# Start and last sequence of a fused Fourier-layer and MLP kernel: whole products and unread ones in the first rounds, a second tile for the mixed rows, a closer step for the last sequence

## The chip, the cores and the metric

The program runs on one core of a Trainium2 chip. The metric is the device time of one execution in microseconds (us), as the median of several runs. TensorE is called PE, VectorE DVE, ScalarE ACT and GpSimd POOL; SP is the engine whose queue issues every DMA of this kernel.

## The reference

Eight sequences of 3136 rows and 256 columns go through a Fourier layer and then a second layer with an MLP, all in fp32:

```python
X = np.fft.rfft(x, axis=1)
Yr = Xr @ w_r - Xi @ w_i + b_r
Yi = Xr @ w_i + Xi @ w_r + b_i
Yr = np.sign(Yr) * np.maximum(np.abs(Yr) - lam, 0.0)     # Yi the same
y = np.fft.irfft(Y, n=x.shape[1], axis=1)
# second layer, x = y
mixed = np.real(np.fft.fft(np.fft.fft(x, axis=1), axis=2))
u = x + mixed
un = (u - mu) / np.sqrt(var + 1e-06)                     # over the 256 columns
out = u + np.maximum(un @ w_ch1, 0.0) @ w_ch2
```

## The kernel before

A sequence of 3136 rows is seen as 64 x 49. Its transform goes in two stages. **F1** (`p1`, `p1_first`) multiplies 64-row slices by a table of cosines and sines and writes the result to DRAM (`ad`; for sequence 0 `a0`, `a8`, `ad0`). **F2** (`p2_f2`, line 531) reads it back as `af`, multiplies it with the table tile `tff`, and splits the result into a high part in fp32r and a remainder (`Xh`, `Xl`, `Xsh`, `Xsl`). A sequence has four quarters q of 8 frequencies u, each with four such products `ui`. **W** (`p2_w`) makes the three complex weight products, 18 matmuls for each half o of the columns. From its result Y one branch (`p2_yt`, `p2_g2`) goes back by the inverse table to DRAM (`bd`), the other (`p2_mix`, tile `mq`) forms the mixed rows and writes them to DRAM (`md`). **G1** (`p3_norm`) reads `bd` as `bf`, ends the inverse transform and adds the mixed rows, read from `md` as `mt`, into `ut`. `p3_tr` transposes `ut`, and `p3_mlp1` and `p3_mlp2` are the MLP (tiles `h` and `o`). A group of the MLP is four (or three) pairs of rows; a sequence has six or seven groups.

Both F1 and G1 contract over 64 rows only, for two halves at once. `quads` writes such a round as four products of 64x64 each, which fill two PSUM tiles; `pair` first clears a column of both tiles by two small DVE memsets (line 322), and `run_quads` (lines 329, 334) lets the products wait for both memsets. A round of F1 of sequence 2 and later can wait in `waiting` for the round of G1 of an older sequence and goes out with it: a joint round. The first sequence uses the whole 128x128 table at once (line 370).

The order is written by a planner: every generator yields virtual times, T = 10000 to a sequence, a heap runs the earliest, and a scheduler then places each engine's instructions. Every engine and SP work their queues in order. Sequence b has its steps of W, mix and G2 at `clock2`, with `STEP` = 0.25 T per quarter (0.13 for sequence 0), and its groups at `clock3`. The MLP weights come as 64-bit floats: `weights` loads them in eight pieces `raw_w` of 512 KB and `split_double` turns each into a pair of fp32r tiles, mostly on DVE (`cv_w`, lines 181 to 199). w1 goes from 1.14 T on in steps of 0.065 T, w2 from 1.73 T on. Pieces 5 and 6 load into the tags `uth` and `utl`, which before hold the split of the odd quarters of sequence 0.

Four PSUM buffers (`gtile`) are shared by all of F1, F2, W, mix, yt, G2, G1 and the transposes; `h` and `o` have two each. `mt` has one buffer and is loaded by four DMAs per group (line 800), `ev` (the result of F1 on its way to DRAM) has four, `im` two.

Of the kernel before, what the change touches and what calls it, by code (L numbers as in the profile page):

```python
# [10 lines left out]
F32 = mybir.dt.float32  # L11
F32R = mybir.dt.float32r
# [15 lines left out]
S = 50  # L28
# [92 lines left out]
T = 10000  # L121
# [7 lines left out]
W_AT, W_STEP = 1.14, 0.065  # L129
W2_AT, W2_STEP = 1.73, 0.07  # L130
MLAG, NRM, TR = 0.874, -1.239, -0.993
TURN = 0.2


@with_exitstack
def spectral_block(ctx: ExitStack, tc: tile.TileContext, x, w_ri, b_ri, w1, w2,
# [31 lines left out]
    UTB, EVB = 7, 4  # L168
# [47 lines left out]
    def load_consts():  # L216
# [6 lines left out]
        wi = sb.tile([128, 2, D], F32, tag="mt", bufs=1, name="wi")  # L223
# [36 lines left out]
    mean_m = cp.tile([128, 128], F32R, name="mean_m")  # L260
    va.memset(mean_m.bitcast(F32), 1.0 / D)
# [76 lines left out]
    def p1_first():  # L338
# [21 lines left out]
        for ci, (m, n) in enumerate(todo):  # L360
# [9 lines left out]
            te.matmul(g[:, :w], fwd_0, xf[:, i * 512:i * 512 + w], start=True, stop=True)  # L370
# [32 lines left out]
    def p1(b):  # L403
# [32 lines left out]
        for k, t in enumerate(times):  # L436
            yield t
            while b == 1 and (0, 1, 1) not in f2_mm:
                yield now[0] + 10
            if k + 1 < len(times):  # L440
                load(k + 1)
            xf = xfs.pop(k)
            if k == 6:
                gs = [gtile("g_f1")]
                te.matmul(gs[0][:, :D], fwd_f, xf[:, :D], start=True, stop=True)
            else:
                gs, marks = pair("g_f1")
                ops = quads(gs, fwd_f, xf.rearrange("q (p i d) -> q p i d", p=2, d=D))
                key = keys[k] if b > 1 else None
                if key is None:  # L450
                    with tc.issue_after(f2_mm[0, 1, 1]) if b == 1 and k == 0 else nullcontext():
                        run_quads(ops, marks)
                else:
                    waiting[key] = ops, marks
                    yield t + 2
                    while key in waiting:
                        yield now[0] + 10
            for r, g in enumerate(gs):
                ev = sb.tile([128, 512], F32, tag="ev", bufs=EVB, name="ev")
                w = D if k == 6 else 512  # L460
                (va.tensor_copy if r else sc.copy)(ev[:, :w], g[:, :w])
                for p in range(2):
                    ad, n2, n = (a_dram[b + p](0)[0], N2 - 1, 1) if k == 6 else (a_dram[b](0)[0], 8 * k + 4 * r + 2 * p, 2)
# [27 lines left out]
    def p2_f2(b):  # L491


        for q in range(4):
# [5 lines left out]
            afs, tfs = [], []  # L500
            for s in range(2):
# [10 lines left out]
                tff = sb.tile([98, 4, 100], F32, tag="eo" if roomy else "tff", bufs=2 if roomy else 3, name="tff")  # L512
                nc.sync.dma_start(out=tff, in_=c_tf[:, u0 + 4 * s:u0 + 4 * s + 4, :])
                afs.append(af)
                tfs.append(tff)
# [3 lines left out]
            for ui in range(4):  # L519
# [34 lines left out]
                else:  # L554
                    im = sb.tile([128, 2, 2 * S], F32, tag="im", bufs=2, name="im")
# [219 lines left out]
    def p3_norm(b):  # L775

        def load_bf(gi):
# [12 lines left out]
        def load_mt(g0, z):  # L790

            mt = sb.tile([128, 4, D], F32, tag="mt", bufs=1, name="mt")
            n0, odd = 2 * g0, g0 + z == NM
            n = 2 * (z - odd)
            for p in range(2):
                for h, (d, back) in enumerate(zip(m_dram[b], (False, True))):
                    v = d[0:NH].rearrange("(a n2) d -> a n2 d", n2=N2)
                    v = v[:, N2 - n0 - n:N2 - n0][:, ::-1] if back else v[:, n0:n0 + n]
                    o = mt[64 * p + 32 * h:64 * p + 32 * h + 32, :n // 2]
                    nc.sync.dma_start(out=o, in_=v.rearrange("a (t p) d -> p a t d", p=2)[p])  # L800
                    if odd:
# [24 lines left out]
        for gi, (g0, z) in enumerate(groups[b % 2]):  # L826
            t0, T3 = clock3(b, g0)
            if gi:
                yield t0 + T3 * (NRM - 0.25)
# [18 lines left out]
            mine = {}  # L848
# [76 lines left out]
    def weights():  # L925
# [13 lines left out]
        yield T * (W_AT - W_STEP)  # L939
# [21 lines left out]
    tasks = [load_small(), load_consts(), weights()]  # L961
# [47 lines left out]
```

## Time and profile before

| | |
|---|---|
| median of 3 runs | 1890.32 us (1889.23 to 1893.35) |
| the profiled execution | 1888.82 us |
| its span, first to last instruction | 1887.0 us |
| PE busy | 1815.6 us (96%) |
| DVE, ACT, POOL busy | 1211.3 us (64%), 820.9 us (44%), 404.9 us (21%) |
| chain that ended last | PE 88%, DMA 5%, DVE 3%, SP's queue 2% |

The page cuts the span in 40 slices; PE is busy 9 tenths or more of each but the first, second and fourth (5, 7 and 5 tenths). So the reader should look at two places, the first 195 us, up to the first product of the MLP, and the few later points at which PE waited. "Granted clock" is the share of PE's full clock that the chip gave in a stretch: 1.00 is 2.4 GHz, 0.50 is 1.2 GHz, and a mean between them is time at either level.

### The profile page before, as it was taken

The page shows a single profiled execution, that of the slowest core. Times are in us where ns is not written, and L with a number is a line of the kernel's source. Part 1 is how long each engine was busy: PE and PEld are TensorE (multiplying, and loading weights), DVE is VectorE, ACT ScalarE, POOL GpSimd, SP SyncE. Part 2 cuts the span into 40 slices and gives each one's busy share as a digit, 9 for nine tenths or more (in the row PEclk, how much of TensorE's full clock was granted, in tenths as well). Part 3 has the DMA queues.
Part 4 walks back from the last instruction along what each step waited for, and adds up shares of the span by engine and source line. Part 5 has one row for each costly group of instructions (what it writes and reads, how often), then busy time and mean ns, then how long its engine had stood idle before and what let it go on. Part 6 is the DMA issues. An engine that isn't in the chain of part 4 may idle for free.

```text
span 1887.0 us, 34092 instructions
## 1 busy us (share of the span) xinstructions
PE 1815.6 (96%) x12344; PEld 1620.0 (86%) x12344; DVE 1211.3 (64%) x2853; ACT 820.9 (44%) x1839; POOL 404.9 (21%) x858
## 2 busy tenths in 40 slices
PE   5795999999999999999999999999999999999999
PEld 3673889989889988898899988988989998987898
DVE  2665777767667766666766676666667666655443
ACT  2564544444445444444444444444444443432222
POOL 0444222222222112322112222211222221211000
PEclk7896999999999999999999999999999999999999
DMA  7768453355345535354354554345435432232110
GB/s 203 206 174 237 131 148 114 102 147 158 102 119 155 153 107 137 103 141 129 102 148 125 158 141 116 92 124 152 120 86 141 126 92 69 68 109 86 53 35 26
DMA packets 155581, 232.94 MB, mean 123 GB/s; under 512 B 19022, under 2 KB 110742, under 8 KB 155414
## 3 DMA queue, kind: packets, MB, share of 16 engines
q1 hardware_dynamic: 155414, 230.78, 44.4%
q8 instruction: 97, 1.59, 0.4%
q14 instruction: 70, 0.57, 0.1%
HBM read 127.95 MB, written 102.76 MB: 122 GB/s over the span
## 4 chain that ended last, share of the span: by engine, by line
PE 88%; DMA 5%; DVE 3%; SPq 2%; issue 1%; ACT 1%; POOL 0%; DVEq 0%; ACTq 0%
PE o L157 10%; PE o L158 9%; PE h L157 9%; PE h L158 9%; PE h L159 9%; PE o L159 9%; PE g_f L531 5%; PE g_w L157 3%; PE g_w L159 3%; PE g_w L158 3%; PE g_yt L727 3%; PE g_ut L877 2%; PE g_g L329 2%; PE g_mix L658 2%; PE g_g L157 1%; PE g_f L334 1%
## 5 line engine op out<-in xcount | busy, mean ns | idle before, releaser
L899 DVE SCALAR_TENSOR_TENSOR hl<-h,hh 128x512 fp32r<-128x512 f32 (+1 forms) x416 | 273.6, 658 | 378.0 <-ACT hh L898 377.0
L898 ACT ACTIVATE hh<-h 128x512 fp32r<-128x512 f32 (+1 forms) x416 | 238.6, 574 | 462.9 <-PE h L159 427.9
L158 PE MATMUL o<-w2h,hl 128*128 128x256 f32 x1568 | 432.2, 285 | 1.2 <-DVE hl L899 1.1
L159 PE MATMUL o<-w2h,hh 128*128 128x256 f32 x1568 | 423.2, 280 | 0.0
L157 PE MATMUL o<-w2l,hh 128*128 128x256 f32 x1568 | 399.9, 288 | 0.0
L157 PE MATMUL h<-utl,w1h 128*128 128x512 f32 (+1 forms) x832 | 323.6, 389 | 0.0
L158 PE MATMUL h<-uth,w1l 128*128 128x512 f32 (+1 forms) x832 | 318.5, 383 | 0.0
L159 PE MATMUL h<-uth,w1h 128*128 128x512 f32 (+1 forms) x832 | 318.2, 382 | 0.0
L157 PEld LDWEIGHTS o<-w2l,hh 128*128 128x128 f32 x1568 | 283.3, 189 | 33.7 <-issue 17.9
L158 PEld LDWEIGHTS o<-w2h,hl 128*128 128x128 f32 x1568 | 296.3, 189 | 7.9 <-issue 2.4
L159 PEld LDWEIGHTS o<-w2h,hh 128*128 128x128 f32 x1568 | 296.5, 189 | 2.8 <-issue 0.8
L817 POOL TENSOR_SCALAR vv<-ag 128x2 f32<-128x2 f32 x104 | 20.5, 197 | 728.8 <-DVE ag L814 714.1
L159 PEld LDWEIGHTS h<-uth,w1h 128*128 128x128 f32 x832 | 156.5, 188 | 23.7
L157 PEld LDWEIGHTS h<-utl,w1h 128*128 128x128 f32 x832 | 157.0, 189 | 17.3 <-DVE hl L899 2.4
L158 PEld LDWEIGHTS h<-uth,w1l 128*128 128x128 f32 x832 | 157.0, 189 | 16.3 <-issue 3.2
L531 PE MATMUL g_f<-tff,af 98*128 98x100 f32 x1024 | 149.9, 281 | 14.9 <-DMA tff<-c_tf 9.4
L531 PEld LDWEIGHTS g_f<-tff,af 98*128 98x128 f32 x1024 | 141.8, 200 | 24.6 <-issue 10.6
L154 POOL TENSOR_TENSOR Xl<-xx,Xh 128x400 fp32r<-128x400 f32 (+1 forms) x96 | 102.0, 1064 | 165.5 <-ACT Xh L545 128.2
L600 ACT ACTIVATE r<-g_w,two_t 128x400 f32<-128x400 f32 x128 | 76.2, 596 | 98.7 <-DVE g_w L596 89.6
L154 POOL TENSOR_TENSOR Xsl<-xs,Xsh 128x200 fp32r<-128x200 f32 x120 | 80.0, 669 | 121.7 <-ACT Xsh L545 116.9
L596 DVE SCALAR_TENSOR_TENSOR g_w<-g_w,bias,ks 128x400 f32<-128x400 f32 x128 | 81.3, 636 | 37.0 <-PE g_w L159 31.0
L673 POOL TENSOR_TENSOR mq<-mq 100x508 f32<-100x508 f32 x31 | 43.5, 1404 | 279.7 <-DVE mq L671 234.1
(155 smaller groups left out, 3364.2 us busy)
## 6 DMA issues: line engine op xcount, KB each, us to landing
bd<-bev SPq DMA_DIRECT2D x128, 196.0 KB
out_dram<-ut SPq DMA_DIRECT2D x92, 256.0 KB
af<-ad SPq DMA_DIRECT2D x60, 392.0 KB
ad<-ev SPq DMA_DIRECT2D x176, 128.0 KB
xf<-in_x SPq DMA_DIRECT2D x86, 256.0 KB
md<-mq SPq DMA_DIRECT2D x112, 192.0 KB
bf<-bd SPq DMA_DIRECT2D x80, 256.0 KB
mt<-md SPq DMA_DIRECT2D x160, 128.0 KB
```

The lines of the kernel that those rows point to most:

```text
L154: gp.tensor_sub(out_, full, hi.bitcast(F32))
L157: te.matmul(o, lh, rl, start=start, stop=False)
L158: te.matmul(o, ll, rh, start=False, stop=False)
L159: return te.matmul(o, lh, rh, start=False, stop=stop)
L329: mm = te.matmul(*ops[0], start=True, stop=True)
L531: f2_mm[b, q, ui] = te.matmul(o, afs[s][:, ui * D + k * 128:ui * D + k * 128 + 128], tfs[s][:, ui].rearrange("p (c j) -> p c j", c=2), sta ...
L596: va.scalar_tensor_tensor(gw, gw, bias[:, c, o:o + 1], ks, op0=ALU.add, op1=ALU.add)
L600: sc.activation(r, gw, AF.Relu, bias=lam_t)
L673: me.tensor_add(mq[:, 0, :, 0, 1:], even[:, :, 1:], odd[:, :, 1:])
L727: te.transpose(gt[:100, (v * 2 + o) * 128:(v * 2 + o + 1) * 128], y[:, o, place].rearrange("p c j -> p (c j)"), ident)
L898: sc.activation(hh[:, :w], h[:, :w], AF.Relu)
L899: va.scalar_tensor_tensor(hl[:, :w], h[:, :w], 0.0, hh[:, :w].bitcast(F32), op0=ALU.max, op1=ALU.subtract)
```

## The change

1. Products that nobody reads: `keep_busy(n)` issues n products of 128x512 of a constant tile into a PSUM tile of tag `o`: 8 ahead of the first F1 product, 14 behind the fourth, 32 behind the last of F1 of sequence 0, and 14 behind F2 of its first quarter, 68 in all.
2. All six F1 rounds of sequence 1, three of sequence 2 and the first group of G1 of sequence 0 use the whole 128x128 table: two products of 128x512 (18 for F1, 2 for G1), without memsets, each with its own evacuation. They come at 1.235 T and on in steps of 0.034 T, the first behind the fourth F2 product of quarter 1 (`FIRST`). Sequence 2 has three early rounds of its own (`EARLY`, before two) and three joint ones (before four).
3. In a joint round ScalarE copies both F1 tiles; before, it copied one and VectorE the other.
4. The first two table tiles `tff` are loaded ahead of the first stores; w1 starts at 1.27 T in steps of 0.055 T.
5. `mt` has two buffers and is loaded half a group's time ahead instead of a quarter; the first group's is loaded in two pieces (8 DMAs of 64 KB), and G1 of that group runs piece by piece. `ev` has three buffers, `im` one.
6. The quarters of the last sequence stand 0.235 T apart instead of 0.25 T.

```diff
-W_AT, W_STEP = 1.14, 0.065
+W_AT, W_STEP = 1.27, 0.055
+EARLY, HALF = (1.66, 1.775, 1.885), 0.058
+FIRST, F1_AT, F1_STEP = (0, 1, 3), 1.235, 0.034
-    UTB, EVB = 7, 4
+    UTB, EVB = 7, 3
+    def load_tf():
+        yield 0.95 * T
+        for s in range(2):
+            tff = sb.tile([98, 4, 100], F32, tag="tff", bufs=3, name="tff")
+            behind("x", out=tff, in_=c_tf[:, 4 * s:4 * s + 4, :])
+            first_tf.append(tff)
+    def keep_busy(n, last=None):
+        o = ps.tile([128, 512], F32, tag="o", bufs=2, name="o_idle").rearrange("p (a k) -> p a k", k=128)
+        m = mean_m.rearrange("p (a k) -> p a k", a=1).to_broadcast((128, 4, 128))
+        for _ in range(n):
+            with tc.issue_after(last) if last is not None else nullcontext():
+                last = te.matmul(o, mean_m, m, start=True, stop=True).ins
...
-            te.matmul(g[:, :w], fwd_0, xf[:, i * 512:i * 512 + w], start=True, stop=True)
+            if ci == 0:
+                keep_busy(8)
+            mm = te.matmul(g[:, :w], fwd_0, xf[:, i * 512:i * 512 + w], start=True, stop=True)
+            if ci == 3:
+                keep_busy(14, mm.ins)
+            if ci == len(todo) - 1:
+                keep_busy(32, mm.ins)
...
-            times = [T * (1.18 + 0.07 * k) for k in range(6)]
+            times = [T * (F1_AT + 2 * F1_STEP * k) for k in range(6)]
-            times = {g1_time(c, gi): (c, gi) for c in range(b) for gi in range(len(groups[c % 2]))}
-            times.update({T * 1.62: None, T * 1.71: None})
+            times = {g1_time(c, gi): (c, gi) for c in range(b) for gi in range(len(groups[c % 2])) if c + gi}
+            times.update({T * t: None for t in EARLY})
...
+            whole = k == 6 or b == 1 or keys[k] is None
...
+                if whole:
+                    yield t + (F1_STEP if b == 1 else HALF) * T * r
+                    g = gtile("g_f1")
+                    with tc.issue_after(f2_mm[FIRST]) if b == 1 and k == r == 0 else nullcontext():
+                        te.matmul(g[:, :w], fwd_f, xf[:, r * 512:r * 512 + w], start=True, stop=True)
-                (va.tensor_copy if r else sc.copy)(ev[:, :w], g[:, :w])
+                (va.tensor_copy if r and whole else sc.copy)(ev[:, :w], g[:, :w])
...
-        step = T * ((STEP0, STEP1)[b] if b < 2 else STEP)
+        step = T * ((STEP0, STEP1)[b] if b < 2 else STEP if b < NB - 1 else 0.235)
-                    im = sb.tile([128, 2, 2 * S], F32, tag="im", bufs=2, name="im")
+                    im = sb.tile([128, 2, 2 * S], F32, tag="im", bufs=1, name="im")
+                if b == q == o == 0:
+                    keep_busy(14, f2_mm[0, 0, 3])
...
-            mt = sb.tile([128, 4, D], F32, tag="mt", bufs=1, name="mt")
+            mt = sb.tile([128, 4, D], F32, tag="mt", bufs=2, name="mt")
+            cuts = (0, 4, 8) if b == g0 == 0 else (0, n)
-                yield t0 + T3 * (NRM - 0.25)
+                yield t0 + T3 * (NRM - 0.5)
+            if b == gi == 0:
+                for i, n in parts_of[z]:
+                    yield max(now[0], g1_time(b, gi) + T3 * i / 4)
+                    g = gtile("g_g1")
+                    with behind_w(1, i == 0):
+                        te.matmul(g, inv_f, bf[:, i * D:i * D + 512], start=True, stop=True)
+                    ut = mine[i] = sb.tile([128, 2, D], F32, tag="ut", bufs=UTB, name="ut")
+                    va.tensor_add(ut, g.rearrange("p (n d) -> p n d", d=D), mt[:, i:i + n])
...
-        yield T * (W_AT - W_STEP)
+        yield T * (W_AT - 2 * W_STEP)
```

How this stands in the built programs is shown at three places. The first is PE's order behind W of quarter 0, first half (sequence 0): `g_f<-tff,af` is F2 of quarter 1, `g_f<-xf` is F1 of sequence 1, `g_w` is W. Before:

```order
L531 MATMUL g_f_395<-tff,af 128x2x50 x4
L531 MATMUL g_f_412<-tff,af 128x2x50 x4
L329 MATMUL g_f_433<-xf,fwd_f 64x512
L334 MATMUL g_f_433<-xf,fwd_f 64x512
L334 MATMUL g_f_432<-xf,fwd_f 64x512 x2
L531 MATMUL g_f_448<-tff,af 128x2x50 x4
L157 MATMUL g_w<-Xsl,wrh 128x400
```

With the change, behind three F2 products (12 matmuls) and the first six matmuls of W:

```order
L159 MATMUL g_w<-Xl,wsh 128x400
L160 MATMUL g_w<-Xh,wsl 128x400
L161 MATMUL g_w<-Xh,wsh 128x400
L159 MATMUL g_w<-Xl,wsh 128x400
L160 MATMUL g_w<-Xh,wsl 128x400
L161 MATMUL g_w<-Xh,wsh 128x400
L561 MATMUL g_f_519<-tff,af 128x2x50 x4
L482 MATMUL g_f_525<-xf,fwd_f 128x512
L159 MATMUL g_w<-Xl,wdh 128x400
```

The first F1 product of sequence 1 now stands behind all four F2 products of quarter 1 and behind 12 matmuls of W, where before it stood behind two F2 products and ahead of W.

The second place is DVE's order where it reaches the first piece of w2 (`raw_w2`); `g_f1` are PSUM tiles of F1 of sequence 2, `mq` the mixed rows of sequence 0. Before:

```order
L322 MEMSET g_f1_1396 128x1
L186 TENSOR_SCALAR cv_w2_ut_1424<-raw_w2_1353 128x512
L322 MEMSET g_f1_1397 128x1
L182 TENSOR_SCALAR cv_w2_hh_1420<-cv_w2_hh_1420 128x512
L677 COPY mq_1133<-mq_1133 100x4x127
```

With the change:

```order
L703 TENSOR_TENSOR mq_1164<-mq_1164 100x4x64 x2
L188 TENSOR_SCALAR cv_w2_ut_1449<-raw_w2_1391 128x512
L184 TENSOR_SCALAR cv_w2_hh_1445<-cv_w2_hh_1445 128x512
L186 TENSOR_SCALAR cv_w2_hh_1445<-cv_w2_hh_1445 128x512
L184 TENSOR_SCALAR cv_w2_hh_1557<-cv_w2_hh_1557 128x512
L189 TENSOR_TENSOR cv_w2_ut_1449<-cv_w2_ut_1449,cv_w2_hh_1445 128x512
L186 TENSOR_SCALAR cv_w2_hh_1557<-cv_w2_hh_1557 128x512
L709 COPY mq_1164<-mq_1164 100x4x127
L700 TENSOR_TENSOR mq_1381<-g_mix_1417,mq_1381 100x1
```

The memset of an F1 tile no longer stands behind the first read of a piece of w2; an evacuation of a mix tile (line 700) still does. On SP the pieces of w2 are issued as 1353, 1355 before and as 1393, 1391 with the change, so the piece that DVE reads first is now the second of the two.

The third place is PE's order ahead of the first transposes of the last sequence (`g_ut<-ident,ut`, which need its mixed rows). Before:

```order
L158 MATMUL h<-uth,w1l 128x512
L159 MATMUL h<-uth,w1h 128x512
L157 MATMUL h<-utl,w1h 128x512
L158 MATMUL h<-uth,w1l 128x512
L159 MATMUL h<-uth,w1h 128x512
L157 MATMUL o<-w2l,hh 128x256 x2
L877 MATMUL g_ut<-ident,ut 128x128 x8
```

With the change:

```order
L159 MATMUL h<-utl,w1h 128x512
L160 MATMUL h<-uth,w1l 128x512
L161 MATMUL h<-uth,w1h 128x512
L159 MATMUL h<-utl,w1h 128x512
L160 MATMUL h<-uth,w1l 128x512
L161 MATMUL h<-uth,w1h 128x512
L923 MATMUL g_ut<-ident,ut 128x128 x8
```

Between the last mix product of the last sequence and these transposes stand 24 matmuls of `h` and 62 of `o` before, 36 and 72 with the change. At the same place of sequence 6 it is 35 of `h`, 47 of `o` and 6 of G2 before, 48, 63 and 12 with the change; at sequences 2 and 4 nothing moves (48, 54 and 6).

## Rows read from the trace of the kernel before

**Rows 1.** Stretches: start:end, us, busy (x) PE, PEld, DVE, ACT, POOL, PEclk, DMA share, GB/s

```profile
0.00:56.00 56.00, 30.68 (x96) 21.04 (x100) 15.81 (x37) 16.18 (x37) 5.87 (x13) 0.77 0.80 210
0.00:194.85 194.85, 135.89 (x654) 103.67 (x655) 107.58 (x231) 91.68 (x220) 73.58 (x86) 0.81 0.77 206
31.48:47.28 15.80, 12.51 (x48) 12.20 (x49) 3.07 (x7) 4.70 (x13) 4.33 (x6) 0.50 0.87 237
1499.00:1510.00 11.00, 9.79 (x64) 9.55 (x65) 7.93 (x25) 4.29 (x11) 2.27 (x11) 0.84 0.79 204
1697.00:1710.00 13.00, 8.88 (x50) 6.96 (x50) 6.07 (x19) 2.65 (x6) 1.65 (x10) 0.87 0.32 89
```

**Rows 2.** Chain that ended last, single steps: start us, us, engine, what, line

```profile
38.55 6.22 DMA af<-a
91.03 0.87 PE g_f L531 x8
95.73 0.61 PE g_f L329
96.39 0.38 PE g_f L329
109.04 0.95 PE g_mean L269 x4
1775.57 0.43 PE g_g L845 x2
```

**Rows 3.** PE in order of time, first 195 us: start, us, what [idle before <-ended by]

```profile
12.87 9.23 PE L370 MATMUL g_f<-xf,fwd 128*128 128x512 f32 x18 [1.91 <-DMA xf<-in_x]
31.48 7.12 PE L531 MATMUL g_f<-tff,af 98*128 98x100 f32 x32 [9.38 <-DMA tff<-c_tf]
41.89 0.70 PE L157 MATMUL g_w<-Xsl,wrh 128*128 128x400 f32 x1 [3.29 <-POOL Xsl L154]
47.78 1.93 PE L531 MATMUL g_f<-tff,af 98*128 98x100 f32 x16
55.71 1.08 PE L329 MATMUL g_f<-xf,fwd_f 64*64 64x512 f32 x1 [6.01 <-ACT xx L550]
68.31 1.14 PE L531 MATMUL g_f<-tff,af 98*128 98x100 f32 x8
138.21 0.34 PE L159 MATMUL g_w<-Xh,wdh 128*128 128x400 f32 x1
149.94 1.11 PE L329 MATMUL g_f<-xf,fwd_f 64*64 64x512 f32 x1 [6.04 <-DVE g_f L322]
194.85 0.39 PE L157 MATMUL h<-utl,w1h 128*128 128x512 f32 x1
```

**Rows 4.** SP's queue and DVE in order of time, around the first piece of w2

```profile
143.73 0.42 SPq L287 DMA_DIRECT2D raw_w<-in_w  x1
149.40 0.43 DVE L186 TENSOR_SCALAR cv_w_ut<-raw_w 128x512 int32<-128x512 int32 x1 [6.66 <-DMA raw_w<-in_w]
```

**Rows 5.** Chain that ended last, from the last mixed rows of sequence 0

```profile
170.80 0.32 SPq L683
178.77 7.48 DMA mt<-md
186.42 1.29 DVE ut L852 x2
```

**Rows 6.** PE in order of time, three of the later waits

```profile
615.74 0.36 PE L157 MATMUL g_g<-yl,tih 100*98 100x256 f32 x1 [0.71 <-DVE ut L852]
1499.38 0.64 PE L727 MATMUL g_yt<-ident,Y 128*100 128x128 f32 x4 [1.36 <-DVE ut L852]
1702.00 1.60 PE L877 MATMUL g_ut<-ident,ut 128*128 128x128 f32 x8 [4.09 <-DVE ut L852]
```

**Rows 7.** Line 461 (evacuation of F1): engine, count, ns min/median/max, first and last start

```profile
L461 ACT COPY ev<-g_f x45: 367/586/589, 57.8 to 1416.6; 128x512 f32<-128x512 f32 x42, 128x256 f32<-128x256 f32 x3
L461 DVE COPY ev<-g_f x42: 656/659/693, 57.7 to 1416.8; 128x512 f32<-128x512 f32 x42
```

More of the change, by code (lines that the diff above doesn't have):

```diff
@@ L222, in load_consts @@
         behind("x", out=KF["wr"], in_=w_v[0])
-        wi = sb.tile([128, 2, D], F32, tag="mt", bufs=1, name="wi")
+        wi = sb.tile([128, 2, D], F32, tag="mt", bufs=2, name="wi")
         behind("x", out=wi, in_=w_v[1])
@@ L249, in load_small @@
         behind("x", out=bias, in_=b_ri)
+    mean_m = cp.tile([128, 128], F32R, name="mean_m")
+    va.memset(mean_m.bitcast(F32), 1.0 / D)
+    def keep_busy(n, last=None):
[4 more added lines that the diff above has]
+                last = te.matmul(o, mean_m, m, start=True, stop=True).ins
     lows = [cp.tile([100, 2, 128], F32, name=f"low{i}") for i in range(2)]
@@ L259, in spectral_block @@
     mlp_w = {}
-    mean_m = cp.tile([128, 128], F32R, name="mean_m")
-    va.memset(mean_m.bitcast(F32), 1.0 / D)
     def center(q):
@@ L442, in p1 @@
             xf = xfs.pop(k)
[L443 to L446, printed above, removed]
+            w = D if k == 6 else 512
+            whole = k == 6 or b == 1 or keys[k] is None
+            if not whole:
                 gs, marks = pair("g_f1")
[L448 to L452, printed above, removed]
-                else:
[L454 to L458, printed above, removed]
+                waiting[keys[k]] = quads(gs, fwd_f, xf.rearrange("q (p i d) -> q p i d", p=2, d=D)), marks
+                yield t + 2
+                while keys[k] in waiting:
+                    yield now[0] + 10
+            for r in range(2 - (k == 6)):
+                if whole:
[3 more added lines that the diff above has]
+                        te.matmul(g[:, :w], fwd_f, xf[:, r * 512:r * 512 + w], start=True, stop=True)
+                else:
+                    g = gs[r]
                 ev = sb.tile([128, 512], F32, tag="ev", bufs=EVB, name="ev")
-                w = D if k == 6 else 512
-                (va.tensor_copy if r else sc.copy)(ev[:, :w], g[:, :w])
+                (va.tensor_copy if r and whole else sc.copy)(ev[:, :w], g[:, :w])
                 for p in range(2):
-                    ad, n2, n = (a_dram[b + p](0)[0], N2 - 1, 1) if k == 6 else (a_dram[b](0)[0], 8 * k + 4 * r + 2 * p, 2)
+                    n2, n = 8 * k + (4 * p + 2 * r if whole else 4 * r + 2 * p), 2
+                    ad = a_dram[b](0)[0]
+                    if k == 6:
+                        ad, n2, n = a_dram[b + p](0)[0], N2 - 1, 1
                     st_eng.dma_start(out=n2_rows(ad, n2, n),
@@ L499, in p2_f2 @@
             xt[b, q] = Xh, Xl, Xsh, Xsl = x_tiles(b, q)
-            afs, tfs = [], []
+            afs, tfs = [], first_tf if b == q == 0 else []
             for s in range(2):
@@ L511, in p2_f2 @@
                     ld = nc.sync.dma_start(out=af, in_=ad[:, :, u:u + 4].rearrange("n c u d -> (n c) (u d)"))
-                tff = sb.tile([98, 4, 100], F32, tag="eo" if roomy else "tff", bufs=2 if roomy else 3, name="tff")
-                nc.sync.dma_start(out=tff, in_=c_tf[:, u0 + 4 * s:u0 + 4 * s + 4, :])
+                if not (b == q == 0):
+                    tff = sb.tile([98, 4, 100], F32, tag="eo" if roomy else "tff", bufs=2 if roomy else 3, name="tff")
+                if not (b == q == 0):
+                    nc.sync.dma_start(out=tff, in_=c_tf[:, u0 + 4 * s:u0 + 4 * s + 4, :])
+                    tfs.append(tff)
                 afs.append(af)
-                tfs.append(tff)
                 if b == 0:
@@ L782, in load_bf @@
                 rows = bf[64 * k:64 * k + 64].rearrange("p (n d) -> p n d", d=D)
+                if b == gi == 0:
+                    nc.sync.dma_start(out=rows, in_=b_dram[0][k:8:2].rearrange("n c u d -> (c u) n d"))
+                    continue
                 n = 4 if z == 4 else 2
@@ L958, in weights @@
                 load(5)
-    tasks = [load_small(), load_consts(), weights()]
+    tasks = [load_tf(), load_small(), load_consts(), weights()]
     for b in range(NB):
```

20 lines of the change are left out of this document (12 added, 8 removed).

## The prediction

> **What bounds the kernel now.** I read the stretches first. Up to the first product of the MLP at 194.85 us PE is busy 135.9 us at a mean granted clock of 0.81 [rows 1, 3]: 59 us idle, and a part of the busy time at 1.2 GHz. Behind that PE is busy but for a few waits, the longest of 4.09 us [rows 6], and the end. So behind 195 us only PE's own work and these waits count; before it a chain of loads, evacuations and stores does, with PE mostly waiting. The second view is PE in order of time, which names the early waits [rows 3]: 9.38 us for the first `af` and `tff`, 3.29 us for POOL's split, 6.01 us ahead of the first F1 round of sequence 1, 6.04 us ahead of a round of sequence 2. From 31.48 to 47.28 the clock is 0.50 throughout [rows 1], behind the 9.38 us of idleness: F2 of quarter 0 takes 7.12 us there for 32 matmuls, where 8 take 0.87 us at full clock [rows 2, 3].
>
> The third view is SP and DVE around 149 us [rows 4]. DVE waits 6.66 us for the first piece of w2, issued at 143.73, and the second memset of an F1 pair stands behind that wait in DVE's order; so PE stands too. The fourth is the chain from the mixed rows of sequence 0: stores from 170.80, the `mt` load to 186.25, `ut` at 186.42, the MLP at 194.85 [rows 3, 5].
>
> **The change part by part.** The sum is made against the profiled execution, 1888.8 us (span 1887.0 and 1.8 around it); the median of the runs is 1.5 above it, and the forecast is given as such a median.
>
> *Price of a whole product.* A round of quads takes 0.61 + 0.38 = 0.99 us for two tiles [rows 2]. Line 845 multiplies 256 columns by the whole table in 0.43 us [rows 2], so 512 columns take 0.86 and two tiles 1.72. Nine F1 rounds and one of G1 thus cost PE 10 x 0.73 = 7.3 us more. All lie ahead of the MLP's first product, where PE has 59 us idle. I charge those of the stretch in which PE is the busier and let the idleness hide the rest.
>
> *Start to 57 us.* The unread products take 0.24 us each at full clock, as the four of line 269 take 0.95 us [rows 2]: 32 are 7.6 us in a gap of 9.38, 14 are 3.3 in gaps of 1.91 and 3.29 [rows 3]. Those behind the fourth F1 product stick out by 1.4 us, but the nine products behind them, 9.23 us with a part at the lower clock, need 8.5 x 0.86 = 7.3, so F1 ends no later. With the clock held, F2 of quarter 0 takes 4 x 0.87 = 3.5 us instead of 7.1. Its first tile is complete after 20 of the 32 matmuls and ACT sets the pace from there, so W starts 5/8 x 3.6 = 2.3 us earlier, and up to 1 more by the table tiles. W's 18 matmuls, 41.89 to 47.78, halve: 2.9. So this half of W ends some 5.5 us earlier, near 42.
>
> Then F2 of quarter 1 waits for its `af`, which landed at 44.77 [rows 2] and comes about 1 us earlier, as two issues ahead of it are gone. PE goes on with F2 and W of what is there, where before it stood 6.01 us ahead of F1 [rows 3]. The bound is then the load of quarter 2's `af`. By the sizes in SP's order 12.1 MB go up to and with it (x 3.2, constants 0.9, stores 3.3, six `af` 2.4, tables 0.8, a piece of w1 0.5, two rounds of x 1.0). The queues moved 56 x 0.210 = 11.8 MB up to 56 us [rows 1]; the rest takes 1.5 us at 237 GB/s, less the microsecond of earlier issue: 57 us. F2 of quarter 2 begins there, against 68.31 [rows 3]: **11 us gained**.
>
> *57 us to the end of W of sequence 0.* Before, this went from 68.31 to 138.5 [rows 3]. Eleven whole products (9.5 us) stand there in place of five rounds (5.0): +4.5. Off it come the waits for two free tiles and two memsets at once, which I take as 2 us. The conversions of w1 still lie in it; DVE is busy 55% and ACT 47% of these 195 us [rows 1], so they have room. Net +2.5: the gain falls to **8.5 us**.
>
> *To the mixed rows.* Two pieces of w2 need the tiles that W frees at 138.5; they were issued 5.2 us later, behind F1's stores [rows 3, 4]. Now they come about 1 us behind W, but DVE reads first the piece issued second, 512 KB more, 2.2 us at 237 GB/s. A mix tile still waits behind that read in DVE's order, so PE still stands there, only not for F1. DVE gets one copy of 0.66 us more ahead of the mixed rows [rows 7]. Between -1 and +4 us of gain; I take **1**, near the row of DVE's own wait.
>
> *Mixed rows to MLP.* Before 24.05 us, 170.80 to 194.85 [rows 3, 5]. The first four loads of `mt` are half as large, and each half of the group goes on by itself: DVE makes one `ut` of 0.65 us instead of two before the first transposes. The load took 7.48 us [rows 5] among 1.2 MB of other loads (`bf`, `af`, tables), and 1 MB is still there. Between 0 and 5; I take **2.5**. So the MLP starts 8.5 + 1 + 2.5 = 12 us earlier, near 183. What is left for PE behind it is the same number of products of each kind, so these 12 us go through to the end.
>
> *Last sequence.* `h` has 512 columns and takes 0.24 us as line 269 does; `o` with 256 half of it. The 0.235 T put 12 `h` and 10 `o` more between the last mix and the transposes: 2.9 + 1.2 = 4.1 us, against 4.09 that PE waits at 1702 [rows 6]; I take 4.0. At 1499 it is 13 `h`, 16 `o` and 6 of G2: 5.8 us of cover against a wait of 1.36. The place becomes like that of sequence 2, which keeps 0.71 [rows 6]; with the short wait behind it, 1.5 us. Both waits are followed by a lower clock, 0.84 over 11 us and 0.87 over 13 us [rows 1]: 1.8 and 1.7 us of PE's time, which come back if the waits end. Sum 4.0 + 1.5 + 3.5 = **9 us**, between 4 and 10.
>
> *The rest.* In the 33 joint rounds ACT copies two tiles, 2 x 0.59 = 1.17 us, and DVE is rid of 0.66 [rows 7]. ACT is the less busy of the two [rows 1], and PE has MLP work queued meanwhile: nothing; a rival prices it. The second `mt` tile takes a wait off SP's queue that PE's work hid. Fewer `ev` and `im` tiles bind only where evacuations follow within a store's time; the early ones stand 0.034 T apart, 7 us with T some 217 us (186.42 to 1702.00 in seven sequences [rows 5, 6]): nothing.
>
> Sum: 1888.8 - 12 - 9 = 1867.8, as a median 1869.
>
> **The rivals.**
> - *The start's gain is given back at w2.* If the pieces of w2 come no earlier, what was gained before is waited for there, and some 4 of the 12 us stay: 1877. For it: the same 20 conversion steps stand ahead of the mixed rows. Against it: the pieces are tied to W, and W comes earlier.
> - *Whole products on the path.* If idleness hides none of the 7.3 us, the start gains 7.3 - 2.5 = 5 less: 1874. For it: PE is busy 136 of the 195 us [rows 1], so some stretches have no gap. The Trainium skill (TensorEngine Tiling (Array Packing), Theoretical Speedup) holds that a contraction of at most 64 rows gains up to twofold when the array is split, which speaks against this part; the rows agree, 0.99 against 1.72 us, and by that rule alone the change would only lose.
> - *The start gains more.* If DVE's wait no longer holds PE at all and the halves of `mt` save their 5 us, 8.5 + 4 + 5 = 17.5: 1863; with no charge for whole products 1860.
> - *The last sequence's step doesn't do what it should.* If `ut` comes 4 us later too, since DVE works in order, the 9 us shrink to 2: 1876.
> - *Slower: the unread products at 1.2 GHz.* They stand in PE's order ahead of real work. If the full clock isn't granted when they run, they take 0.48 us each: 32 are 15.4 us in a gap of 9.38, twice 14 are 6.7 in 1.91 and 3.29 [rows 3]: 6.0 + 4.8 + 3.4 = 14 us late, and nothing is gained up to 57 us; with the 7.3 us of whole products on the path the start loses 21 and the end gains 9: 1902. It is decided by the clock when the fourth F1 product ends, near 11 us. Against it: the waits before are now filled.
> - *ACT in the joint rounds.* If each of 33 rounds held the MLP up by 0.59 us, 19 us would be lost, and the whole would come out within 0.2% of before. Against it: queued `h` products cover it.
>
> **How the numbers follow.** Forecast (1862 to 1873) 0.50; given back at w2 0.16; whole products on the path 0.08; more 0.12; last step without effect 0.05; slower 0.05; ACT 0.04. The range takes in all but the last two and the outer edges: 1857 to 1884. A measurement of this kernel tells about 0.2%, 4 us, from no change. Faster by more than that 0.91, within it 0.04, slower 0.05.
>
> **What would show it.** Right: clock 1.00 up to 50 us; F2 of quarter 0 in 3.5 us; F2 of quarter 2 at 57; first `h` near 183; no wait over 1 us behind 1400. Wrong: unread products at 0.48 us each; PE waiting 5 us or more for w2 again; the wait ahead of the last sequence's transposes still there; new waits on `hh` behind joint rounds.

## The result and the profile of the changed kernel

| | before | changed |
|---|---|---|
| median, beside each other | 1889.78 us (1887.51 to 1893.35) | 1867.34 us (1866.29 to 1868.68) |
| ratio | | 0.9879, 95% interval 0.9864 to 0.9895 |
| profiled execution, its span | 1888.82 us, 1887.0 us | 1868.68 us, 1866.9 us |
| first product `h` of the MLP | 194.85 us | 183.39 us |
| from there to the end | 1692.15 us | 1683.51 us |
| PE idle ahead of the first `h` | 59.0 us | 37.4 us |

The change saves 22.4 us in the median. The forecast was 1869 us with a range of 1857 to 1884. In the traces 11.5 us come ahead of the first `h` and 8.6 us behind it, 20.1 together; forecast were 12 and 9. So both halves of the sum hold, as far as one trace of each kernel can tell. Most of the terms that make up the first half do not, as the rest of this document shows.

The stretches of the changed kernel stand first (start:end, us, busy (x) PE, PEld, DVE, ACT, POOL, PEclk, DMA share, GB/s). They answer to [rows 1].

```profile
0.00:56.00 56.00, 42.56 (x169) 30.92 (x170) 14.99 (x34) 15.65 (x36) 6.56 (x13) 0.89 0.82 209
0.00:183.39 183.39, 146.00 (x683) 113.13 (x683) 102.87 (x209) 90.94 (x221) 69.46 (x84) 0.89 0.80 214
183.39:1866.90 1683.51, 1675.25 (x11691) 1513.38 (x11690) 1081.64 (x2593) 745.44 (x1651) 330.43 (x775) 1.00 0.42 115
1477.00:1488.00 11.00, 11.00 (x89) 9.94 (x88) 6.99 (x19) 4.82 (x12) 3.24 (x4) 1.00 0.72 203
1660.00:1690.00 30.00, 27.80 (x188) 23.45 (x187) 15.27 (x42) 8.31 (x19) 5.15 (x17) 1.00 0.66 175
```

Behind the first `h` PE now idles 1683.51 - 1675.25 = 8.3 us, 4.2 in four short waits and the rest at the end, and its clock is 1.00. The two places at which PE waited for `ut` at a lower clock are gone: the stretches at 1477 and 1660 us answer to those at 1499 and 1697 of [rows 1].

PE in order of time, as in [rows 3], shows the start:

```profile
1.05 3.78 PE L271 MATMUL o_idle<-mean_m 128*128 128x512 f32 x8 [1.05 <-DVE mean_m L263]
...
8.82 3.76 PE L271 MATMUL o_idle<-mean_m 128*128 128x512 f32 x14
...
21.39 7.63 PE L271 MATMUL o_idle<-mean_m 128*128 128x512 f32 x32
30.22 3.79 PE L561 MATMUL g_f<-tff,af 98*128 98x100 f32 x32 [1.20 <-DMA af<-a]
33.78 3.45 PE L271 MATMUL o_idle<-mean_m 128*128 128x512 f32 x14
39.41 0.45 PE L159 MATMUL g_w<-Xsl,wrh 128*128 128x400 f32 x1 [2.17 <-POOL Xsl L156]
...
44.33 1.95 PE L561 MATMUL g_f<-tff,af 98*128 98x100 f32 x16
53.93 2.03 PE L561 MATMUL g_f<-tff,af 98*128 98x100 f32 x8 [7.64 <-DVE Y L633]
...
61.78 1.14 PE L561 MATMUL g_f<-tff,af 98*128 98x100 f32 x8
...
132.35 0.35 PE L161 MATMUL g_w<-Xh,wdh 128*128 128x400 f32 x1
...
163.11 0.70 PE L159 MATMUL g_w<-Xsl,wrh 128*128 128x400 f32 x1 [6.87 <-POOL Xsl L156]
...
183.39 0.39 PE L159 MATMUL h<-utl,w1h 128*128 128x512 f32 x1
```

The unread products take 0.24 us each, at full clock. F2 of quarter 0 takes 3.8 us where it took 7.12. The granted clock up to 56 us is 0.89 in the mean (0.77 before), not the 1.00 up to 50 us that the forecast named as a sign of being right. Then comes a wait that the forecast did not have: 7.64 us until 53.93. VectorE in order of time says what it is, and behind it ScalarE:

```profile
42.77 0.64 DVE L628 SCALAR_TENSOR_TENSOR g_w<-g_w,bias,ks 128x400 f32<-128x400 f32 x1 [4.01 <-issue]
52.09 0.43 DVE L188 TENSOR_SCALAR cv_w_ut<-raw_w 128x512 int32<-128x512 int32 x1 [8.67 <-DMA raw_w<-in_w]
...
53.30 0.57 DVE L633 SCALAR_TENSOR_TENSOR Y<-g_w,r 128x400 f32<-128x400 f32 x1
```

```profile
40.80 0.49 ACT L620 COPY ks<-g_w 128x400 f32<-128x400 f32 x1 [2.13 <-PE g_w L161]
52.09 0.67 ACT L183 ACTIVATE cv_w_hh<-raw_w 128x512 f32<-128x512 f32 x1 [10.79 <-DMA raw_w<-in_w]
```

Both engines stand at the first piece of w1 until it lands at 52.09. The evacuations of W and F2 are queued behind it, so PE finds no free tile and stands too.

The trace of the kernel before has this wait as well, at 51.31 us. VectorE before, and behind it ScalarE before:

```profile
51.31 0.43 DVE L186 TENSOR_SCALAR cv_w_ut<-raw_w 128x512 int32<-128x512 int32 x1 [4.31 <-DMA raw_w<-in_w]
```

```profile
51.31 0.68 ACT L181 ACTIVATE cv_w_hh<-raw_w 128x512 f32<-128x512 f32 x1 [6.53 <-DMA raw_w<-in_w]
...
53.67 0.67 ACT L181 ACTIVATE cv_w_hh<-raw_w 128x512 f32<-128x512 f32 x1 [0.82 <-DMA raw_w<-in_w]
...
55.24 0.48 ACT L550 COPY xx<-g_f 128x400 f32<-128x400 f32 x1
```

The last of these copies is the one that ended PE's 6.01 us ahead of F1 [rows 3]. It stood behind two pieces of w1 in ScalarE's order.

### The profile page after: what moved, and what is told of

Its sections match the earlier page's. It is cut to its first block, busy times and chain, and to the rows that moved or that the text cites. A ratio compares the mean times of both kernels' runs of the same rounds, so it can differ in the third digit from the quotient of the medians.

```text
span 1866.9 us, 34114 instructions
## 1 busy us (share of the span) xinstructions
PE 1821.3 (98%) x12372; PEld 1626.5 (87%) x12372; DVE 1184.5 (63%) x2800; ACT 836.4 (45%) x1872; POOL 399.9 (21%) x858
## 4 chain that ended last, share of the span: by engine, by line
PE 90%; DMA 5%; SPq 2%; DVE 1%; issue 1%; ACT 0%; POOL 0%; DVEq 0%; POOLq 0%; ACTq 0%
PE o L159 10%; PE h L159 10%; PE h L160 10%; PE o L160 10%; PE h L161 10%; PE o L161 10%; PE g_f L561 5%; PE g_w L159 4%; PE g_w L161 3%; PE g_w L160 3%; PE g_yt L759 3%; PE g_g L349 2%; PE g_ut L923 2%; PE g_mix L690 2%; PE g_g L159 1%; PE g_f L354 1%
## 5 line engine op out<-in xcount | busy, mean ns | idle before, releaser
L159 PEld LDWEIGHTS o<-w2l,hh 128*128 128x128 f32 x1568 | 282.8, 189 | 33.5 <-issue 17.1
L561 PE MATMUL g_f<-tff,af 98*128 98x100 f32 x1024 | 144.0, 273 | 10.8 <-DVE Y L633 7.6
L561 PEld LDWEIGHTS g_f<-tff,af 98*128 98x128 f32 x1024 | 135.7, 193 | 16.8 <-DVE Y L633 7.8
```

The source lines that it names most:

```text
L159: te.matmul(o, lh, rl, start=start, stop=False)
L561: f2_mm[b, q, ui] = te.matmul(o, afs[s][:, ui * D + k * 128:ui * D + k * 128 + 128], tfs[s][:, ui].rearrange("p (c j) -> p c j", c=2), sta ...
```

## The experiments

Every kernel below is the changed one with one edit. Medians are of several executions beside the kernel before; "against changed" is the difference to 1867.34 us. The runs were made in four sittings, in which the kernel before took 1888.3 to 1889.8 us in the median, so the ratios compare better than the medians. The interval of a ratio is some 0.3% wide; two ratios are told apart when they differ by some 0.2%, which is 4 us. The changed kernel has 0.9879.

| run | median, us | against changed | ratio to before, 95% interval |
|---|---|---|---|
| no_unread | 1872.58 | +5.2 | 0.9911, 0.9893 to 0.9928 |
| step_025 | 1876.06 | +8.7 | 0.9932, 0.9915 to 0.9948 |
| quads_early | 1874.88 | +7.5 | 0.9919, 0.9904 to 0.9934 |
| w1_behind | 1868.85 | +1.5 | 0.9890, 0.9873 to 0.9906 |
| joint_split | 1865.74 | -1.6 | 0.9879, 0.9862 to 0.9895 |
| one_mt | 1865.73 | -1.6 | 0.9880, 0.9866 to 0.9895 |
| group_quads | 1867.02 | -0.3 | 0.9884, 0.9869 to 0.9899 |
| w1_times | 1870.88 | +3.5 | 0.9905, 0.9891 to 0.9920 |
| quads_seq1 | 1876.68 | +9.3 | 0.9928, 0.9916 to 0.9941 |
| quads_seq2 | 1868.61 | +1.3 | 0.9885, 0.9871 to 0.9898 |
| start_undone | 1881.27 | +13.9 | 0.9951, 0.9939 to 0.9964 |
| w1_later | 1868.00 | +0.7 | 0.9883, 0.9867 to 0.9899 |

### The unread products

```diff
-        for _ in range(n):
+        for _ in range(0):
```

> All 68 unread products are left out; every product whose result is used stays. As the prediction put it, the clock is worth 5.5 us at the end of W's first half and carries F2 of quarter 2 with it: the first h near 188 us, the whole near 1872, 5 us above the changed kernel. The theory from the trace of the changed kernel: DVE and ACT stand at the first piece of w1 until 52.09 us whatever the clock before was, so F2 of quarter 0 takes 7 us again, W's first half ends near 48 and not at 44.3, but PE goes on at 53.9 as before: first h within 1 us of 183.4, the whole 1866 to 1869.

Measured: 1872.58 us, +5.2. The size is that of the forecast's view; the marks up to 54 us are those of the theory drawn from the changed trace, whose total falls. F2 of quarter 0 takes 7.12 us again from 31.08 on, and W's first half ends at 47.5 and not at 44.5. Yet PE goes on behind the wait for w1 at 53.99 us, as in the changed kernel at 53.93:

```profile
31.08 7.12 PE L561 MATMUL g_f<-tff,af 98*128 98x100 f32 x32 [9.05 <-DMA af<-a]
...
53.99 2.03 PE L561 MATMUL g_f<-tff,af 98*128 98x100 f32 x8 [4.74 <-DVE Y L633]
```

So the size is right, but the way there is not shown: at 54 us the two kernels are level, and the first `h` comes at 185.45, 2.1 us later, where the first view had 5 and the second 1 at most. Another 2.3 us are lost behind it, 1685.85 us to the end against 1683.51. PE's order is the same but for the unread products; SP, DVE and ACT have a few instructions in other places. Which of this carries the 5.2 us stays open.

### The step of the last sequence

```diff
-else 0.235)
+else STEP)
```

> Only the step of the last sequence goes back to 0.25 T. Theory: the wait for ut ahead of its transposes near 1680 us is back with 3 to 4 us, the one near 1480 with about 1 us, both followed by a lower clock; first h unmoved at 183.4; the whole 7 to 9 us above the changed kernel, 1874 to 1877. Rival: the 8.65 us that the stretch behind the first h gained came from ACT's copies in the joint rounds or the second mt tile; then at most 3 us are lost, 1867 to 1870.

Measured: 1876.06 us, +8.7, as the theory has it. PE in order of time has the waits back:

```profile
1484.64 0.64 PE L759 MATMUL g_yt<-ident,Y 128*100 128x128 f32 x4 [1.74 <-DVE ut L898]
...
1487.01 0.38 PE L160 MATMUL o<-w2h,hl 128*128 128x256 f32 x1 [0.82 <-DVE hl L945]
...
1687.52 1.97 PE L923 MATMUL g_ut<-ident,ut 128*128 128x128 f32 x8 [3.92 <-DVE ut L898]
```

These are 6.5 us of waiting; the rest is clock (0.74 in the 13 us from 1685 on). From the first `h` at 179.78 to the end this run takes 1693.1 us, 9.6 more than the changed kernel. The copies and the `mt` tile, which were left in, give nothing there: the rival falls.

### The whole products

```diff
-            whole = k == 6 or b == 1 or keys[k] is None
+            alone = k == 6 or b == 1 or keys[k] is None
+            whole = k == 6
...
-                waiting[keys[k]] = quads(gs, fwd_f, xf.rearrange("q (p i d) -> q p i d", p=2, d=D)), marks
+                ops = quads(gs, fwd_f, xf.rearrange("q (p i d) -> q p i d", p=2, d=D))
+                if alone:
+                    with tc.issue_after(f2_mm[FIRST]) if b == 1 and k == 0 else nullcontext():
+                        run_quads(ops, marks)
+                else:
+                    waiting[keys[k]] = ops, marks
...
```

> The nine F1 rounds made of whole products (six of sequence 1, three early ones of sequence 2) go back to quads with two memsets, at the changed kernel's times. Price by PE alone: 9 x 0.73 = 6.6 us less work. Theory: that work lies in idle time, and the memsets stand again behind DVE's waits for pieces of w1 and w2; PE's busy time up to the first h falls by some 6 us, but the first h comes 0 to 5 us later, the whole 1867 to 1872. Rival (whole products on the path): the first h comes 3 to 6 us earlier, the whole 1861 to 1864.

Measured: 1874.88 us, +7.5, more than the theory's upper end; the first `h` comes at 189.45. The rival, which forecast a gain, falls. Two halves of this edit followed. `whole = k == 6 or b > 1 and keys[k] is None` turns back only the six rounds of sequence 1:

> Only the six F1 rounds of sequence 1 are quads with memsets; the three early rounds of sequence 2 stay whole. With all nine as quads the last weight product of sequence 0 ended at 137.1 us and not at 129 to 133, and the rest was lost behind it. Theory: a pair needs two free tiles and two memsets at once in a stretch where every tile waits for an evacuation, so it is lost wherever such rounds stand: 4 to 5 us here, the whole near 1872, the last weight product near 136. Rival: all is lost at the pieces of w2, and these six cost nothing or give PE's 4.4 us back: 1863 to 1868.

Measured: 1876.68 us, +9.3, twice the theory's price. `whole = k == 6 or b == 1` turns back only the three of sequence 2:

> Only the three early rounds of sequence 2 are quads with memsets; the six of sequence 1 stay whole. Theory: the last weight product of sequence 0 stays at 129 to 133 us, 2 to 4 us are lost behind it, at the read of the first piece of w2 that stands ahead of the memsets in DVE's order: the whole near 1870. Rival: the loss of the nine is all of this place: near 1875, with PE waiting 4 us or more for a memset or an evacuation between 140 and 160.

Measured: 1868.61 us, +1.3: next to nothing, less than either expected. The nine, the six and the three (7.5, 9.3 and 1.3 us) fit together within the noise: the six rounds of sequence 1 carry the loss. The one stretch 61.78 to 132.70 us, F2 of quarter 2 to the last weight product in the changed kernel, shows what is lost with the six rounds; the columns are those of the first fence, the changed kernel stands first, then `quads_seq1`:

```profile
61.78:132.70 70.92, 64.29 (x340) 52.76 (x340) 49.61 (x98) 45.28 (x113) 35.45 (x42) 0.93 0.68 187
```

```profile
61.78:132.70 70.92, 57.57 (x324) 44.84 (x325) 49.31 (x103) 42.52 (x105) 30.77 (x36) 0.89 0.65 169
```

PE's idle time doubles, from 6.6 to 13.4 us; `quads_early` has 13.3 there. The lower clock of 0.89 is not shown to come from the rounds: `quads_early` has 0.93, as the changed kernel. The profiled execution of `quads_seq1` was the slowest of its five, 1878.56 us. PE in order of time in `quads_seq1` has these waits among others; line 349 is the first product of a round, line 342 its memset:

```profile
71.57 1.51 PE L567 MATMUL g_f<-tff,af 98*128 98x100 f32 x8 [2.80 <-ACT ks L626]
...
76.44 0.70 PE L159 MATMUL g_w<-Xl,wdh 128*128 128x400 f32 x1 [1.87 <-DVE xs L589]
...
127.67 1.11 PE L349 MATMUL g_f<-xf,fwd_f 64*64 64x512 f32 x1 [3.39 <-DVE g_f L342]
...
139.56 0.34 PE L161 MATMUL g_w<-Xh,wdh 128*128 128x400 f32 x1
```

The last weight product ends at 139.90 and not at 132.70, and the first `h` comes at 193.41. Only one of the listed waits is for a memset, though; the others are for evacuations. What these stood behind is in the queues of ScalarE and VectorE in `quads_seq1`:

```profile
70.47 0.66 ACT L183 ACTIVATE cv_w_hh<-raw_w 128x512 f32<-128x512 f32 x1 [3.08 <-DMA raw_w<-in_w]
71.04 0.48 ACT L626 COPY ks<-g_w 128x400 f32<-128x400 f32 x1
```

```profile
122.58 3.86 DVE L715 COPY mq<-mq 100x508 f32<-100x508 f32 x1
...
127.56 0.06 DVE L342 MEMSET g_f<- 128x1 f32 x1
```

The copy `ks` stood behind a piece of w1, the memset behind a long copy of the mixed rows. The changed kernel has both as well: its ScalarE waits 2.48 us for a piece of w1 until 68.67, and the copy takes 3.50 us from 116.92 on. PE loses less by them there. That a round of quads takes two of the four PSUM tiles at once, so that the products behind it find none while an evacuation is late, fits these rows, but it is not shown: no run gave the kernel more tiles. The Trainium skill (TensorEngine Tiling (Array Packing), Restrictions and Gotchas) says that row tiling increases the pressure on PSUM. The traces agree so far as the waits above are for evacuations and a memset.

### The first piece of w1

The first conversion of w1 is put behind F2 of quarter 1 in ScalarE's and VectorE's order (`held` are its last copy and its last subtraction there):

```diff
-        sc.activation(tf, hi.bitcast(F32), AF.Abs)
+        with tc.issue_after(held[0]) if held else nullcontext():
+            sc.activation(tf, hi.bitcast(F32), AF.Abs)
...
-        va.tensor_scalar(w, hi, -0x80000000, 0x40000000, op0=ALU.bitwise_and, op1=ALU.bitwise_or)
+        with tc.issue_after(held[1]) if held else nullcontext():
+            va.tensor_scalar(w, hi, -0x80000000, 0x40000000, op0=ALU.bitwise_and, op1=ALU.bitwise_or)
+        held.clear()
...
         load(0)
+        yield from after("x1")
```

> The changed kernel, with the first conversion of w1 put behind F2 of quarter 1 in the order of ACT and of DVE, so that no evacuation of W of quarter 0 or of F2 of quarter 1 waits for the first piece of w1; nothing else is moved by hand. Theory: PE's idle 7.64 us until 53.93 falls below 2 us, F2 of quarter 2 begins at 56 to 58 us and not at 61.78 (then bound by its af load), and 2 to 5 us of it come out at the first h: the whole 1862 to 1865. Rival: what is gained is waited for at the pieces of w1 and w2 later, and the first h stays at 183: 1866 to 1869.

Measured: 1868.85 us, no gain: the rival holds. The wait is gone, and F2 of quarter 2 begins at 57.58 us, just where the forecast had put it:

```profile
44.33 2.45 PE L565 MATMUL g_f<-tff,af 98*128 98x100 f32 x20 [1.09 <-DMA tff<-c_tf]
...
53.14 2.05 PE L486 MATMUL g_f<-xf,fwd_f 128*128 128x512 f32 x2 [3.26 <-DMA xf<-in_x]
...
57.58 1.15 PE L565 MATMUL g_f<-tff,af 98*128 98x100 f32 x4 [0.40 <-DMA tff<-c_tf]
...
76.17 0.70 PE L159 MATMUL g_w<-Xs,wrh 128*128 128x400 f32 x1 [3.05 <-DVE Y L641]
```

But W of quarter 1 is done at 88.95 us, against 89.34 in the changed kernel, and the first `h` comes at 183.63. So the 4 us gained by 58 are gone by 89. The edit moved one load too: the third piece of w1 is issued at 68.78 us, in the changed kernel at 60.06. In between DVE is nearly full, as the stretch 62 to 90 us of this run shows, with the columns of the first fence:

```profile
62.00:90.00 28.00, 24.17 (x113) 18.93 (x112) 25.65 (x45) 17.11 (x39) 16.29 (x15) 0.82 0.64 179
```

DVE is busy 25.65 of 28 us there (24.20 in the changed kernel, 18.96 before). The conversions, put off, meet the evacuations of two quarters. That DVE sets the pace here is read from this row; no run took work from it.

### The planned times of w1

```diff
-W_AT, W_STEP = 1.27, 0.055
+W_AT, W_STEP = 1.14, 0.065
-        yield T * (W_AT - 2 * W_STEP)
+        yield T * (W_AT - W_STEP)
```

> Only the planned times of w1 go back, to 1.14 T and steps of 0.065 T. SP then issues two pieces of w1 ahead of the af of quarter 2, 512 KB more, 2.2 us at 231 GB/s. The prediction put nothing on these times: 1866 to 1869. A theory in which the early loads set the pace gives F2 of quarter 2 at 64 and not at 61.78 and 2 us more in the whole, 1868 to 1871. If the start is paced further on instead, as the run with w1 behind F2 of quarter 1 suggests, the first h stays within 1 us of 183.4.

Measured: 1870.88 us, +3.5, with F2 of quarter 2 at 60.31 us. By the ratios the loss is 0.26%, just beyond the noise. So the times seem to count, but not in the way expected: the load of quarter 2 is not late. W of quarter 1 ends at 90.99 us, and between 62 and 90 PE is busy 21.34 us, against 23.59. ScalarE and VectorE stand at the third piece of w1 until 67.65 us in this run, 4.69 and 2.65 us long:

```profile
67.65 0.68 ACT L183 ACTIVATE cv_w_hh<-raw_w 128x512 f32<-128x512 f32 x1 [4.69 <-DMA raw_w<-in_w]
```

In the changed kernel ScalarE's longest wait for a piece there is 2.48 us. Whether this is all that holds PE was not told apart. The other direction, `W_AT, W_STEP = 1.35, 0.05` with the first load kept at 1.16 T, was a try at a faster kernel:

> A try at a faster kernel: w1 still loads its first piece at 1.16 T, but its conversions are planned at 1.35 T and in steps of 0.05 T, later than 1.27 T and 0.055 T. Undoing the change's own delay cost 3.5 us. If the direction goes on, the second to fourth piece load behind the af of quarters 2 and 3 and another 1 to 3 us are gained: 1864 to 1866. If the means of w1 (two products of mean_m) then stand late ahead of w2, it is even or slower: 1867 to 1871.

Measured: 1868.00 us, the same as the changed kernel. The last weight product comes at 129.29, but 33.5 us then pass to the first store of the last mixed rows, where the changed kernel needs 28.2.

### Three edits without effect

```diff
-                (va.tensor_copy if r and whole else sc.copy)(ev[:, :w], g[:, :w])
+                (va.tensor_copy if r else sc.copy)(ev[:, :w], g[:, :w])
```

> Only the copies of the joint rounds go back: VectorE takes the second F1 tile, ScalarE the first; the early rounds stay as they are. Theory: 33 copies lie under the MLP's queued products on either engine, so nothing moves by more than 2 us: 1866 to 1869, with the stretch behind the first h as long as before, 1682 to 1685 us. Rival: ScalarE's two copies in a row hold the MLP up, and without them the whole falls by 3 to 10 us; or VectorE's relief is part of the 8.65 us gained there, and the whole rises by 3 to 5 us.

```diff
-        wi = sb.tile([128, 2, D], F32, tag="mt", bufs=2, name="wi")
+        wi = sb.tile([128, 2, D], F32, tag="mt", bufs=1, name="wi")
...
-            mt = sb.tile([128, 4, D], F32, tag="mt", bufs=2, name="mt")
+            mt = sb.tile([128, 4, D], F32, tag="mt", bufs=1, name="mt")
...
-                yield t0 + T3 * (NRM - 0.5)
+                yield t0 + T3 * (NRM - 0.25)
```

> The mixed rows go back to one tile, loaded a quarter of a group's time ahead. Theory: PE's queued work hid the loads before and hides them still: 1866 to 1869, no new wait for ut over 0.8 us outside the last sequence. Rival: with the last sequence's groups closer, the load of mt comes late there, the wait ahead of its transposes is back with 1 to 4 us, and the whole is 2 to 6 us longer.

```diff
-                if b == gi == 0:
-                    nc.sync.dma_start(out=rows, in_=b_dram[0][k:8:2].rearrange("n c u d -> (c u) n d"))
-                    continue
...
-            cuts = (0, 4, 8) if b == g0 == 0 else (0, n)
+            cuts = (0, n)
...
-            if b == gi == 0:
+            if b < 0:
...
-            run_quads(quads(gs, inv_f, bf[:, :(2 * z - 4) * D].rearrange("q (i p d) -> q p i d", p=2, d=D)), marks, (b, gi))
+            with behind_w(1, b == gi == 0):
+                run_quads(quads(gs, inv_f, bf[:, :(2 * z - 4) * D].rearrange("q (i p d) -> q p i d", p=2, d=D)), marks, (b, gi))
```

> The first group of sequence 0 goes back to one G1 round of quads with two memsets and to four mt loads of 128 KB; all else as in the changed kernel. Theory: from the first store of the last mixed rows to the first h it takes some 2.5 us longer, between 0 and 5: first h near 186, the whole 1868 to 1872. Rival: bf and mt land when they do, since the DMA engines are nearly full there, and the split saves nothing: within 1 us of 1867.3.

Measured: 1865.74, 1865.73 and 1867.02 us. By the ratios that is 0.00, 0.01 and 0.05% off the changed kernel: none of the three parts is worth anything that can be told. For the first two the theory holds, for `group_quads` the rival. From the first `h` to the end the first two take 1682.7 and 1683.2 us, as long as the changed kernel. In `group_quads` the last mixed rows are stored from 157.28 us on and the first `h` comes at 180.24, 22.96 us later; in the changed kernel it is 160.88 and 22.51. So the loads of `mt` in two pieces save half a microsecond at most.

### The three parts of the start together

The edits of no_unread, quads_early and w1_times in one kernel.

> The three parts that cost time when undone singly are undone together: no unread products (5.2 us), nine F1 rounds as quads (7.5), w1 at its old times (3.5). Theory: they are the whole gain of the start and overlap little: the whole at 1879 to 1884, the first h near 194, and only the last sequence's 8.7 us are left against the kernel before. Rival: they share one cause, the loads that set the pace up to 62 us, and together lose no more than the largest: 1875 to 1877.

Measured: 1881.27 us, +13.9, as the theory has it; the first `h` comes at 194.62, the kernel before has it at 194.85. So within the noise these three parts are the whole gain of the start, and 13.9 of the 22.4 us in all; the last sequence's step, 8.7 us by its own run, is the rest. Singly they cost 5.2, 7.5 and 3.5, together 16.2. The 2 us of overlap are not told from none.

## Why the prediction was right, and where it was not

In order of the prediction's steps, with the terms of the start as the two traces give them:

| stretch | before | changed | gain | forecast |
|---|---|---|---|---|
| to F2 of quarter 2 | 68.31 | 61.78 | 6.5 | 11 |
| to the end of W of sequence 0 | 70.24 | 70.92 | -0.7 | -2.5 |
| to the first store of the last mixed rows | 32.25 | 28.18 | 4.1 | 1 |
| to the first `h` | 24.05 | 22.51 | 1.5 | 2.5 |
| sum | 194.85 | 183.39 | 11.5 | 12 |

Each term is read from one trace. `step_025` has the same instructions in the same order up to the last sequence's step, and its trace gives gains of 7.7, 1.7, 2.7 and 2.9 us, 15.1 in all. So a term here is good to some 2.5 us.

- *The clock.* Right for the products that it names: unread products at 0.24 us, F2 of quarter 0 in 3.8 us (forecast 3.5). It was not 1.00 throughout. W's first half ended at 44.5 us in the changed kernel's profile, its clock falling on the way, and at 42.2 to 42.8 in six of the other profiles with the unread products; forecast was near 42. Undone, the part costs 5.2 us, and the forecast gave W's half 5.5. That the two agree confirms nothing: the lead of W's half was gone at 54 us.
- *F2 of quarter 2 at 57.* Wrong by 4.8 us. The failing step is "PE goes on with F2 and W of what is there". It took the 6.01 us wait ahead of F1 [rows 3] for a matter of F1's place in the order. Its releaser was an ACT evacuation, and the reader should have asked what ACT and DVE waited for: the first piece of w1. The trace of before had it, 6.53 and 4.31 us until 51.31, and the changed trace has it until 52.09. The load of `af`, which the step priced, does allow 57: `w1_behind` begins there. But that run also shows that the start to 57 us did not set the end.
- *Whole products cost 2.5 us net.* Wrong in sign by the experiment: with the six rounds of sequence 1 as quads again the changed kernel loses 9.3 us. The traces alone would not tell it, -0.7 us for this stretch in the table and +1.7 in `step_025`. The prices of PE's work hold; the 2 us taken off for waits for two free tiles were mis-sized. The quads of the experiment stand at the changed kernel's times, so it prices the two forms there and not at the times of before. The rival "whole products on the path" falls with it, and the sentence that the change would only lose by the rule of the split array as well.
- *w2.* Forecast 1 us, bounds -1 to 4; 4.1 in the trace. The reason, that the pieces of w2 come sooner behind W, holds, and its size was taken too small. The first piece is issued 0.8 us ahead of W's end, where the forecast had 1 us behind it and before it was 5.2. DVE's wait for the piece that it reads first ends 6.5 us behind W instead of 10.9, and is 2.99 us long instead of 6.66 [rows 4]. That the memsets of sequence 2 no longer stand behind this read has little part in it: `quads_seq2` puts them back and costs 1.3 us, with 29.4 us for this stretch. With the rounds of sequence 1 as quads it takes 32.6 to 33.5 (`quads_seq1`, `quads_early`, `start_undone`), with whole ones 28.2 to 29.6 in nine traces of ten. So this gain goes with the whole rounds of sequence 1, but not with them alone: `w1_later` keeps them and takes 33.5. DVE's wait in the changed kernel:

```profile
139.21 0.43 DVE L188 TENSOR_SCALAR cv_w_ut<-raw_w 128x512 int32<-128x512 int32 x1 [2.99 <-DMA raw_w<-in_w]
```

- *Mixed rows to the MLP.* Forecast 2.5, 1.5 in the trace, and 0.3 in the whole when undone. The bounds, 0 to 5, held it.
- *Last sequence.* Right: 9 forecast, 8.7 measured by its own run, waits and clock both. Not foreseen was a new wait of 1.65 us in the profile of the changed kernel at 1668.03, for `bf`; the forecast had named no wait over 1 us behind 1400 as a sign of being right.
- *The rest.* Joint copies and the second `mt` tile at nothing: right. The times of w1, which were not priced at all, are worth 3.5 us by their own run, just beyond the noise.

So the gain of the last sequence was right by its mechanism, and that of the start by luck: some 3 to 4.5 us too much gain up to 57 us met two terms that were set too low by about as much, the stretch of the whole products and w2.

## What to carry to other kernels

Ask of a waiting engine's releaser what it waited for itself, before moving work around the wait. Here the split of the array saved PE time that PE did not need: six rounds of whole products, with more work for PE, were 9.3 us faster than six of quads. Price such a split by the waits around it and not by PE's time alone, and try it both ways. A wait that is gone (7.64 us, in `w1_behind`) need not be a gain; look at the busy share of the next engine in the stretch behind.

## What the runs showed of the hardware that was not expected

The start of one program differs between executions by several microseconds. `step_025` has the changed kernel's instructions in the same order far beyond the first `h`, yet PE went on at 52.10 us and not at 53.93, and the first `h` came at 179.78 and not at 183.39. In `quads_seq1` F2 of quarter 0 took 6.24 us and not 3.79, though its instructions are those of the changed kernel until behind 57 us. The clock differs too: between 31 and 46 us it was 0.89 in `step_025` and the changed kernel and 1.00 in `quads_early`, whose instructions on PE, DVE, ACT and SP are theirs up to there. So a mark in a single trace is good to some 4 us here, and the medians decide.
